# Pacing the first forty loads of an attention and feed-forward kernel: eight in flight or three

## The chip, the cores and the metric

The kernel runs on one core of a Trainium2 chip. The metric is the device time of one execution in microseconds, lower is better. A core has TensorE (matrix products), VectorE, ScalarE, GpSimd, and SyncE, which here only issues DMA transfers; sixteen DMA engines move the data. Each engine works through its own instructions in order, and engines wait for each other, and for transfers, by semaphores.

## The reference

Attention in two forms on 8 batches of 8 heads (576 positions, head size 64), their sum taken as 4608 tokens of 512 numbers, and a feed-forward block with `h * cos(h)` in the middle. Cut to what matters:

```python
q_d, k_d, v_d = (a.reshape(B, H, S // 4, 4, D).mean(axis=3) for a in (q, k, v))
out_up = np.repeat(sm_attn(q_d, k_d, v_d), 4, axis=2)          # attention on 144 positions
mask = np.abs(pos[:, None] - pos[None, :]) < 4                 # and within three positions
scores = np.where(mask, scale * q @ k.T, -1e9)
out_local = softmax(scores) @ v
x = (out_up + out_local).transpose(0, 2, 1, 3).reshape(4608, 512)
h = x @ w_in                                                   # 512 -> 2048
return (h * np.cos(h)) @ w_out                                 # 2048 -> 512
```

The weights come in float64.

## The kernel before

**Work and stages.** The attention is cut into 32 units, one for each of the 8 batches and 4 pairs of heads. A unit loads q and k (128 x 584 numbers, 292 KB each), v for the averaged form (`vdn`, 288 KB on 72 partitions) and v for the local form (`vl`, 384 KB); then come scores, softmax, transposes and the product with v. The five steps are `u_qk`, `u_v`, `u_s`, `u_t` and `u_pv`. The feed-forward part takes tokens in 12 tiles of 384 and the 2048 inner columns in 16 chunks of 128. Each chunk has one load of `w_in` (`wdi`, 512 KB) and one of `w_out` (`wdo`, 512 KB) in `w_load`, and `w_split` turns the float64 bits into two float32 parts, on ScalarE first (L412) and then on VectorE and GpSimd. `gemm1` (L731) and `gemm2` (L767) are the two products. The first three token tiles go through the chunks in four groups of four, so that the products can begin before all weights are there; the other nine take all chunks at a time.

**What sets the order.** A planner (`Plan`) records every step with an estimate of its length, schedules all steps by list over the engines, and then emits the instructions in that order. The loads have an order by hand: q and k of batch 0 (loads 1 to 8), v of its first two head pairs (9 to 12), weight chunk 0 (13, 14), v of the other pairs (15 to 18), chunk 1 (19, 20), q and k of batch 1 (21 to 28), chunk 2 (29, 30), v of batch 1 (31 to 38), and so on; load 40 is the first q of batch 2. Batches 0 and 1 use memory that later holds weights, so their tiles appear as wxi, wxo and xxl in the rows.

**What the change and the rows touch.** All transfers that SyncE issues pass the helper `dma` (L382 to L385): weights at L402, q and k at L468, vdn at L489, vl at L490, and also moves of `ptb` (L631) and stores of results (L789), which come after the first forty. Of the readers, L482 (VectorE) and L475 and L477 (GpSimd) sum q or k over four positions, L496 and L497 do so for v, and L538 and L547 are the score products. L884 are dummy products that keep TensorE busy in the early part.

**Semaphores.** The framework below the planner puts the waits in. A SyncE transfer signals one of eight semaphores in turn, DMAHW0 to DMAHW7, and before one is taken again SyncE waits for the transfer that had it: at most eight are in flight.

Of the kernel before, what the change touches and what calls it, by code (L numbers as in the profile page):

```python
# [49 lines left out]
ON_PE = ()  # L50
BOOST = {0: 100.0}
LAG = 2
PI = math.pi


# [22 lines left out]
class Plan:  # L78
# [47 lines left out]
    def part(self, parent, off, n, make):  # L126

        b = self.buf(make)
        b.parent, b.prev = parent, []
        for lo, hi, p in parent.parts:  # L130
            if lo < off + n and off < hi:
                b.prev.append(p)
        parent.parts = [x for x in parent.parts if not (off <= x[0] and x[1] <= off + n)] + [(off, off + n, b)]
        return b
# [152 lines left out]
def _act(n, psum=True, extra=0):  # L287
    return n * 0.000833 + (0.051 if psum else 0.093) + 0.093 * extra


def _dve(n):
    return n * 0.001042 + 0.065
# [7 lines left out]
def attn_ffn_kernel(ctx: ExitStack, tc: tile.TileContext, qT, kT, vdn, vl, w_in, w_out, out):  # L300
# [8 lines left out]
    pl = Plan()  # L309

    def sb(tag, n, shape, dtype=F32, name=None, pool=None):
        t = pl.turn(tag, n)
        return pl.buf(lambda: (pool or ap).tile(shape, dtype, name=name or tag, tag=t, bufs=1), t)
# [63 lines left out]
    w_dram = {"i": w_in.bitcast(I32).rearrange("(a p) (f t) -> p a f t", p=P, t=2),  # L377
              "o": w_out.bitcast(I32).rearrange("f (n t) -> f n t", t=2)}

    loads = {}  # L380

    def dma(nbytes, fn, r=(), w=(), pw=()):  # L382
        o = pl.op("SP", max(0.45, nbytes / 262e3), fn, r=r, w=w, pw=pw, lat=1.8)
        loads.setdefault((pl.name,) + pl.arg, []).append(o)
        return o  # L385

# [7 lines left out]
    def w_load(k, c):  # L394
        pl.name = "w_load"
        wd = words[(k, c)]
        if k == "i":
            src = lambda: w_dram["i"][:, :, c * P:(c + 1) * P, :]
            dst = lambda: wd.get().rearrange("p (a f) t -> p a f t", a=KC)
        else:  # L400
            src, dst = (lambda: w_dram["o"][c * P:(c + 1) * P]), wd.get
        dma(4096 * P, lambda: sp.dma_start(dst(), src()), w=[wd])  # L402
# [58 lines left out]
    def u_qk(b, pr):  # L461
        pl.name = "u_qk"
        q, k, qkd = (ub(b, pr, n) for n in ("q", "k", "qkd"))
        s4 = [lambda: q.get()[:, 0:S].rearrange("p (a r) -> p a r", r=4), lambda: k.get()[:, PAD:PAD + S].rearrange("p (a r) -> p a r", r=4)]
        early = b < NEARLY
        bk = bank(b, "t") if early and ON_PE else None
        for i, (src, ram) in enumerate(((q, qT), (k, kT))):
            dma(4 * P * SP_, lambda src=src, ram=ram: sp.dma_start(src.get(), ram[b, pr]), w=[src])  # L468

            def on_pe(i=i):  # L470
                for r in range(4):
                    pe.matmul(bk.get()[:, i * SD:(i + 1) * SD], ident, s4[i]()[:, :, r], start=(r == 0), stop=(r == 3))

            def on_pool(i=i):
                pool.tensor_tensor(out=qkd.get()[:, i], in0=s4[i]()[:, :, 0], in1=s4[i]()[:, :, 1], op=ALU.add)  # L475
                for r in (2, 3):
                    pool.tensor_tensor(out=qkd.get()[:, i], in0=qkd.get()[:, i], in1=s4[i]()[:, :, r], op=ALU.add)  # L477
            if early and i in ON_PE:
                pl.op("PE", 4 * _mm4(SD), on_pe, r=[src], pw=[bk])
                evac(SD, lambda i=i: qkd.get()[:, i], lambda i=i: bk.get()[:, i * SD:(i + 1) * SD], bk, qkd)  # L480
            else:
                pl.op("DVE", _dve(S), lambda i=i: dve.tensor_reduce(out=qkd.get()[:, i], in_=s4[i](), axis=AX.X, op=ALU.add),  # L482
                      r=[src], pw=[qkd], alts=[("POOL", 3 * _pool(2 * SD), on_pool)])
        st[(b, pr)] = dict(q=q, k=k, qkd=qkd)

    def u_v(b, pr):
        pl.name = "u_v"
        vd4, vt = ub(b, pr, "vd4"), ub(b, pr, "vl")
        dma(16 * P * HD * 2, lambda: sp.dma_start(vd4.get(), vdn[b, pr].rearrange("p a r n -> p (a r) n")), w=[vd4])  # L489
        dma(4 * P * 12 * D, lambda: sp.dma_start(vt.get(), vl[b, pr]), w=[vt])  # L490
        vd = ub(b, pr, "vd")
        v4 = lambda: vd4.get().rearrange("p (a r) n -> p a r n", a=2)

        def v_add(e):
            def f():
                e.tensor_tensor(out=v4()[:, :, 0:2, :], in0=v4()[:, :, 0:2, :], in1=v4()[:, :, 2:4, :], op=ALU.add)  # L496
                e.tensor_tensor(out=vd.get(), in0=v4()[:, :, 0, :], in1=v4()[:, :, 1, :], op=ALU.add)  # L497
            return f
        pl.op("POOL", 2.2, v_add(pool), w=[vd, vd4], alts=[("DVE", 1.1, v_add(dve))], shares=True)
        st[(b, pr)].update(vd=vd, vl=vt)  # L500

    def u_s(b, pr):
# [96 lines left out]
        for sm, part, size in ((sml, sul, n), (smd, sud, m)):  # L599
            if not (early and sm is smd):  # L600
                pl.op("DVE", _dve(size), lambda sm=sm, part=part: dve.tensor_reduce(  # L601
                    out=part(), in_=sm.get(), axis=AX.X, op=ALU.add), r=[sm, su], pw=[su2])
        pl.op("DVE", 0.1, lambda: dve.tensor_scalar(out=su.get(), in0=su.get(), scalar1=1e-9, scalar2=2.0 * PI,
                                                    op0=ALU.add, op1=ALU.mult), r=[su2], w=[su])
# [114 lines left out]
    def gemm1(t, c):  # L719
# [15 lines left out]
        tr = sb("tr", 4, [P, m], pool=fp)  # L735
        gh, gl = sb("gh", LAG + 1, [P, m], F32R, pool=fp), sb("gl", LAG + 1, [P, m], F32R, pool=fp)
        h = lambda: ph.get()[:, :m]

        def sin2():
            act.activation(tr.get(), tr.get(), AF.Sin, scale=PI)  # L740
            act.activation(tr.get(), tr.get(), AF.Square)  # L741
# [13 lines left out]
    def gemm2(t, c, c0, c1):  # L755
# [19 lines left out]
        for i in range(SIZE[t] // P):  # L775
# [4 lines left out]
            if c == c1 - 1:  # L780
                bk, ob = accs[i], sb("tr", 4, [P, DM], name="ob", pool=fp)

                pl.op("ACT", _act(DM), lambda bk=bk, ob=ob: act.activation(ob.get(), bk.get(), AF.Copy, scale=-4.0 * PI),
                      r=[bk], w=[ob], alts=[("DVE", _dve(DM), lambda bk=bk, ob=ob: dve.tensor_scalar(
                          out=ob.get(), in0=bk.get(), scalar1=-4.0 * PI, scalar2=None, op0=ALU.mult))])
                dst = out[FROM[t] + i * P:FROM[t] + (i + 1) * P, :]
# [11 lines left out]
    def at(t, f, *a):  # L798
        ev.append((t, len(ev), f, a))

    def unit(t, step, ahead, *a):
        for d, f in ((-ahead, u_qk), (0.01 - ahead, u_v), (0.0, u_s), (step, u_t), (2 * step, u_pv)):
            at(t + d, f, *a)
# [23 lines left out]
    for b in range(2, B):  # L827
        t0, t1 = tile_of(b * S), tile_of(b * S + S - 1)
        lo, hi = (done[t1 - NX] if t1 >= NX else 0), first[t0]
        for i in range(NPAIR):  # L830

            last = max(lo - 2.5 + (hi - lo - 1.0) * i / (NPAIR - 1), last + 1.5)
            unit(last, 1.4, 2.5, b, i)
    for i in range(len(steps) + LAG):
        if i < len(steps):
            at(i, gemm1, *steps[i][:2])
        if i >= LAG:
            at(i + 0.5, gemm2, *steps[i - LAG])
    for t, i, f, a in sorted(ev, key=lambda e: e[:2]):
# [85 lines left out]
```

## Time and profile before

| what | value |
|---|---|
| median of 3 runs | 1016.51 us (1007.5 to 1016.57) |
| profiled execution, its own time | 1012.63 us |
| span of the profiled execution | 1010.8 us |
| TensorE busy | 984.4 us (97%) |
| VectorE, ScalarE, GpSimd busy | 679.4, 610.4, 220.2 us |
| DMA | 80.70 MB, mean 80 GB/s |
| mean granted TensorE clock | 0.986 |

The span runs from the first to the last instruction of one profiled execution. A row of the timeline gives start and length in microseconds, engine, line, operation and tiles; a bracket behind it gives the idle time of that engine just before and what ended it. SPq is SyncE's queue, where the length is that of the issue and not of the transfer; PE is TensorE, DVE is VectorE, ACT is ScalarE, POOL is GpSimd. A row by stretches gives, for each engine, busy microseconds and instructions, then the granted share of TensorE's clock, the mean busy share of the DMA engines, and what they moved.

### The profile page before, as it was taken

How to read it: one execution, taken by the hardware profiler on the slowest of the kernel's cores; microseconds unless marked ns; L12 is line 12 of the kernel's file. 1: busy time of each engine (PE TensorE's matmuls, PEld its weight loads, DVE VectorE, ACT ScalarE, POOL GpSimd, SP SyncE). 2: the span in 40 equal slices, each digit the busy share in tenths (PEclk: the TensorE clock that was granted, in tenths of full speed). 3: DMA queues.
4: the chain of work that ended last, by engine and by line, in shares of the span. 5: the costliest groups of instructions: out<-in, count | busy, mean ns of one | idle time of the engine just before them, and what ended most of it. 6: DMA issues, size and time to landing. Idle time of an engine off the chain costs nothing.

```text
span 1010.8 us, 23855 instructions
## 1 busy us (share of the span) xinstructions
PE 984.4 (97%) x9917; PEld 849.5 (84%) x9917; DVE 679.4 (67%) x1362; ACT 610.4 (60%) x1174; POOL 220.2 (22%) x280
## 2 busy tenths in 40 slices
PE   7888999999999999999999999999999999999998
PEld 4556799899887888888888888888898888899997
DVE  6599899996487678564748866655657875433433
ACT  2457688876576656555647655655646755655554
POOL 5676324623144202100003211200001300000000
PEclk9998799999999999999999999999999999999999
DMA  9753651524255422211212321201112320100000
GB/s 279 232 198 96 231 208 41 86 48 70 52 124 123 83 61 83 67 29 32 67 49 75 121 64 52 88 26 36 58 57 64 112 73 1 40 1 1 32 1 32
DMA packets 41051, 80.70 MB, mean 80 GB/s; under 512 B 4976, under 2 KB 16240, under 8 KB 40944
## 3 DMA queue, kind: packets, MB, share of 16 engines
q1 hardware_dynamic: 37056, 72.11, 22.8%
q0 software_dynamic: 3888, 7.08, 4.9%
q8 instruction: 78, 1.28, 0.5%
q14 instruction: 29, 0.24, 0.1%
HBM read 57.93 MB, written 16.52 MB: 74 GB/s over the span
## 4 chain that ended last, share of the span: by engine, by line
PE 88%; DVE 5%; DMA 3%; POOL 1%; issue 1%; SPq 1%; ACT 1%; ACTq 0%; DVEq 0%; POOLq 0%
PE bank L767 38%; PE bank L731 38%; PE bank L531 2%; PE bank L547 2%; PE bank L676 2%; PE bank L657 2%; PE bank L884 2%; PE bank L640 1%; DMA q<-qT 1%; DMA wdi<-w_in 1%; PE bank L669 1%; PE bank L538 1%; SPq L631 1%; DVE su L601 0%; DMA ptb<-sml 0%
## 5 line engine op out<-in xcount | busy, mean ns | idle before, releaser
L767 PE MATMUL bank<-wo,gh 128*128 128x512 f32 x1152 | 363.6, 396 | 0.0
L767 PEld LDWEIGHTS bank<-wo,gh 128*128 128x128 f32 x1152 | 210.0, 188 | 38.0 <-issue 3.3
L767 PE MATMUL bank<-wo,gl 128*128 128x512 f32 x576 | 227.6, 395 | 0.0
L742 ACT ACTIVATE tr<-bank,bmagic 128x384 f32<-128x384 f32 x192 | 110.9, 577 | 114.7 <-PE bank L731 110.8
L746 DVE SCALAR_TENSOR_TENSOR tr<-tr,bank 128x384 f32<-128x384 f32 x192 | 104.9, 546 | 107.9 <-ACT tr L741 107.1
L743 DVE SCALAR_TENSOR_TENSOR tr<-tr,bank 128x384 f32<-128x384 f32 x192 | 105.7, 550 | 85.2 <-ACT tr L742 84.3
L740 ACT ACTIVATE tr<-tr 128x384 f32<-128x384 f32 x192 | 100.7, 524 | 76.3 <-DVE tr L743 75.7
L748 ACT ACTIVATE gh<-tr 128x384 fp32r<-128x384 f32 x163 | 85.3, 523 | 87.1 <-DVE tr L746 85.5
L391 DVE TENSOR_TENSOR gl<-tr,gh 128x384 fp32r<-128x384 f32 x154 | 92.4, 600 | 63.5 <-ACT gh L748 60.5
L767 PEld LDWEIGHTS bank<-wo,gl 128*128 128x128 f32 x576 | 108.0, 188 | 23.5
L731 PE MATMUL bank<-x0h,wi 128*128 128x384 f32 x384 | 108.0, 342 | 0.0
L731 PE MATMUL bank<-x1h,wi 128*128 128x384 f32 x384 | 107.3, 340 | 0.0
L731 PE MATMUL bank<-x2h,wi 128*128 128x384 f32 x384 | 106.8, 339 | 0.0
L731 PE MATMUL bank<-x3h,wi 128*128 128x384 f32 x384 | 106.5, 338 | 0.0
L741 ACT ACTIVATE tr<-tr 128x384 f32<-128x384 f32 x192 | 100.8, 525 | 6.1
L391 POOL TENSOR_TENSOR gl<-tr,gh 128x384 fp32r<-128x384 f32 x38 | 43.2, 1137 | 268.7 <-DVE gh L749 175.1
L731 PEld LDWEIGHTS bank<-x0h,wi 128*128 128x128 f32 x384 | 70.9, 190 | 2.7 <-DVE mxd L574 0.4
L731 PEld LDWEIGHTS bank<-x1h,wi 128*128 128x128 f32 x384 | 70.6, 189 | 2.6 <-issue 0.6
L731 PEld LDWEIGHTS bank<-x2h,wi 128*128 128x128 f32 x384 | 70.2, 188 | 2.3 <-issue 0.4
L731 PEld LDWEIGHTS bank<-x3h,wi 128*128 128x128 f32 x384 | 70.2, 188 | 2.0
L731 PE MATMUL bank<-x0l,wi 128*128 128x384 f32 x192 | 65.0, 339 | 1.0 <-DVE x0l L391 1.0
L731 PE MATMUL bank<-x1l,wi 128*128 128x384 f32 x192 | 64.7, 337 | 0.0
(199 smaller groups left out, 1452.9 us busy)
## 6 DMA issues: line engine op xcount, KB each, us to landing
vl<-vl SPq DMA_DIRECT2D x26, 384.0 KB
out<-ob SPq DMA_DIRECT2D x36, 256.0 KB
wdi<-w_in SPq DMA_DIRECT2D x16, 512.0 KB
wdo<-w_out SPq DMA_DIRECT2D x16, 512.0 KB
q<-qT SPq DMA_DIRECT2D x26, 292.0 KB
k<-kT SPq DMA_DIRECT2D x26, 292.0 KB
vd<-vdn SPq DMA_DIRECT2D x26, 288.0 KB
out<-ob POOLq DMA_DIRECT2D x27, 256.0 KB, 5.2
```

Of the source, the lines that this page charges most:

```text
L391: f = lambda e: lambda: e.tensor_tensor(out=out(), in0=in0(), in1=in1(), op=ALU.subtract)
L531: pe.matmul(banks[h].get()[BS * g:BS * (g + 1), c:c + BS], q.get()[hs, o:o + BS], k.get()[hs, o:o + BS], start=True, stop=True)
L547: pe.matmul(banks[h].get()[:HD, i * SD:(i + 1) * SD], qkd.get()[hs, 0, i * HD:(i + 1) * HD], qkd.get()[hs, 1, :], start=True, stop=True)
L657: pe.matmul(banks[0].get()[64 * h:64 * h + 64, 2 * SD:3 * SD], vd.get()[:, kh, 64 * h:64 * h + 64], ptd.get()[:, h, kh, :], start=(kh == 0 ...
L731: pe.matmul(ph.get()[:, :m], w[:, i, kc, :], x[:, kc, :], start=(n == 0), stop=(n == 3 * KC - 1))
L740: act.activation(tr.get(), tr.get(), AF.Sin, scale=PI)
L741: act.activation(tr.get(), tr.get(), AF.Square)
L742: pl.op("ACT", _act(m, True, 1), lambda: act.activation(tr.get(), h(), AF.Identity, bias=bmagic), r=[ph], w=[tr])
L743: pl.op("DVE", _dve(m), lambda: dve.scalar_tensor_tensor(out=tr.get(), in0=tr.get(), scalar=MAGIC, in1=h(), op0=ALU.subtract, op1=ALU.subt ...
L746: pl.op("DVE", _dve(m), lambda: dve.scalar_tensor_tensor(out=tr.get(), in0=tr.get(), scalar=0.5, in1=h(), op0=ALU.subtract, op1=ALU.mult), ...
L748: pl.op("ACT", _act(m, False), lambda: act.activation(gh.get(), tr.get(), AF.Copy), r=[tr], w=[gh], alts=[("DVE", _dve(m / 2), lambda: dve ...
L767: pe.matmul(o, (gh, gh, gl)[k].get()[:, sl], wo.get()[:, (0, 1, 0)[k]], start=(c == c0 and k == 0), stop=(c == c1 - 1 and k == 2))
```

## The change

Each of the first forty loads, from the fourth on, gets a dependence on the load three places ahead of it in the order of issue. SyncE waits for that load's semaphore and then issues. From load 41 on the framework's own waits are all there is. The order of instructions on each engine stays as it was.

```diff
+AHEAD, FIRST = 3, 40
...
-    loads = {}
+    loads, begun = {}, []
 
     def dma(nbytes, fn, r=(), w=(), pw=()):
-        o = pl.op("SP", max(0.45, nbytes / 262e3), fn, r=r, w=w, pw=pw, lat=1.8)
+        def begin():
+            ins = fn()
+            if ins is not None and len(begun) < FIRST:
+                if len(begun) >= AHEAD:
+                    tc.add_manual_dep(ins.ins, begun[-AHEAD].name, mybir.DependencyInfo(
+                        mybir.DependencyClass.Sync, mybir.DependencyReason.DATA), reason="loads in flight")
+                begun.append(ins.ins)
+        o = pl.op("SP", max(0.45, nbytes / 262e3), begin, r=r, w=w, pw=pw, lat=1.8)
         loads.setdefault((pl.name,) + pl.arg, []).append(o)
         return o
```

SyncE's queue at the start of the program, before the change, is as follows. The number behind a tile's name tells buffers apart, and the bracket names the semaphores that the issue waits for.

```order
L468 DMA q<-qT 128x584
L468 DMA k<-kT 128x584
L468 DMA wxi_132<-qT 128x584
L468 DMA wxo_136<-kT 128x584
L468 DMA wxo_197<-qT 128x584
L468 DMA wxi_200<-kT 128x584
L468 DMA wxi_214<-qT 128x584
L468 DMA wxo_273<-kT 128x584
L489 DMA vd_281<-vdn 72x1024 [waits DMAHW0_49]
L490 DMA vl<-vl 128x768 [waits DMAHW1_49]
L489 DMA wxi_308<-vdn 72x1024 [waits DMAHW2_49]
```

The same place on SyncE after the change (lines stand eight further down in the changed file):

```order
L476 DMA q<-qT 128x584
L476 DMA k<-kT 128x584
L476 DMA wxi_132<-qT 128x584
L476 DMA wxo_136<-kT 128x584 [waits DMAHW0_49]
L476 DMA wxo_197<-qT 128x584 [waits DMAHW1_49]
L476 DMA wxi_200<-kT 128x584 [waits DMAHW2_49]
L476 DMA wxi_214<-qT 128x584 [waits DMAHW3_49]
L476 DMA wxo_273<-kT 128x584 [waits DMAHW4_49]
L497 DMA vd_281<-vdn 72x1024 [waits DMAHW5_49]
L498 DMA vl<-vl 128x768 [waits DMAHW6_49]
L497 DMA wxi_308<-vdn 72x1024 [waits DMAHW7_49]
```

No row moved. The wait of load 9 was on load 1 and is on load 6, and loads 4 to 8 have a wait where they had none.

SyncE's queue around load 40 before the change, with buffers to be free (PE_49, Pool_49) among the waits:

```order
L490 DMA wxo_585<-vl 128x768 [waits DMAHW5_49,PE_49]
L402 DMA wdi_1049<-w_in 128x4x256 [waits DMAHW6_49]
L468 DMA q<-qT 128x584 [waits DMAHW7_49,Pool_49]
L468 DMA k<-kT 128x584 [waits DMAHW0_49]
L402 DMA wdo_1163<-w_out 128x1024 [waits DMAHW1_49]
L402 DMA wdi_1175<-w_in 128x4x256 [waits DMAHW2_49]
L402 DMA wdo_1202<-w_out 128x1024 [waits DMAHW3_49]
```

And the same place after the change:

```order
L498 DMA wxo_585<-vl 128x768 [waits DMAHW2_49,PE_49]
L410 DMA wdi_1049<-w_in 128x4x256 [waits DMAHW3_49]
L476 DMA q<-qT 128x584 [waits DMAHW4_49,Pool_49]
L476 DMA k<-kT 128x584
L410 DMA wdo_1163<-w_out 128x1024
L410 DMA wdi_1175<-w_in 128x4x256
L410 DMA wdo_1202<-w_out 128x1024
```

Load 40 (q) waits for load 37 in place of load 32, and loads 41 to 45 need no wait of their own any more, since the loads eight ahead of them are known to have landed.

## The prediction

> **What bounds the kernel now.** I read the page's shares first, then the work by stretches of time, then SyncE's queue (where the change is made), and last the instructions that use the loads. The page, engines and chain:
>
> ```profile
> span 1010.8 us, 23855 instructions
> PE 984.4 (97%) x9917; PEld 849.5 (84%) x9917; DVE 679.4 (67%) x1362; ACT 610.4 (60%) x1174; POOL 220.2 (22%) x280
> PE 88%; DVE 5%; DMA 3%; POOL 1%; issue 1%; SPq 1%; ACT 1%; ACTq 0%; DVEq 0%; POOLq 0%
> ```
>
> TensorE is busy 97% of the span, so a change can reach at most 1010.8 - 984.4 = 26.4 us of idle time there, and that busy time includes dummy matmuls early on. The view by stretches (per engine busy us and count, then granted clock, DMA share, GB/s) shows where the idle lies:
>
> ```profile
> 0.00:5.00 5.00, 3.63 (x16) 1.15 (x20) 1.38 (x3) 1.28 (x1) 3.90 (x16) 1.00 0.63 196
> 5.00:10.00 5.00, 5.00 (x206) 3.04 (x206) 2.74 (x8) 0.02 (x1) 4.32 (x16) 1.00 1.03 350
> 20.00:25.00 5.00, 5.00 (x73) 2.81 (x67) 2.35 (x7) 0.61 (x2) 0.39 (x1) 0.66 1.03 250
> 30.00:35.00 5.00, 4.38 (x118) 2.74 (x117) 4.96 (x13) 3.31 (x14) 1.72 (x2) 1.00 1.01 360
> 35.00:40.00 5.00, 4.13 (x51) 2.16 (x49) 5.00 (x12) 1.85 (x5) 2.53 (x4) 1.00 0.68 197
> 40.00:60.00 20.00, 16.44 (x346) 10.21 (x339) 13.63 (x23) 6.42 (x15) 18.25 (x27) 0.91 0.30 87
> 120.00:1011.00 891.00, 884.14 (x7876) 783.19 (x7874) 585.84 (x1175) 550.84 (x1008) 151.65 (x173) 1.00 0.23 63
> ```
>
> From 120 us on TensorE idles only 6.9 us in 891; the first sixty microseconds hold the forty loads, and the DMA engines are full (share 1.0) from 5 to 35 us. So the change acts where the transfers are saturated, and reaches the end only through what waits for a load there.
>
> SyncE's queue before, as the timeline has it (start, length, instruction):
>
> ```profile
> 0.74 0.39 SPq L468 DMA_DIRECT2D q<-qT  x1
> 1.65 0.43 SPq L468 DMA_DIRECT2D wxi<-qT  x1
> 2.12 0.43 SPq L468 DMA_DIRECT2D wxo<-kT  x1
> 4.02 0.54 SPq L468 DMA_DIRECT2D wxo<-kT  x1
> 5.76 0.32 SPq L489 DMA_DIRECT2D wxi<-vdn  x1
> 7.20 0.33 SPq L490 DMA_DIRECT2D wxo<-vl  x1
> 7.92 0.38 SPq L402 DMA_DIRECT2D wdi<-w_in  x1
> 8.66 0.34 SPq L402 DMA_DIRECT2D wdo<-w_out  x1
> 9.57 0.32 SPq L489 DMA_DIRECT2D wxo<-vdn  x1
> 10.86 0.33 SPq L490 DMA_DIRECT2D wxi<-vl  x1
> 22.14 0.33 SPq L468 DMA_DIRECT2D xxl<-qT  x1
> 57.54 0.32 SPq L489 DMA_DIRECT2D wxi<-vdn  x1
> 58.85 0.46 SPq L468 DMA_DIRECT2D q<-qT  x1
> ```
>
> The kernel is already paced, at eight: load n+8 waits for the semaphore of load n, so where nothing else holds it, the issue of load n+8 tells when load n landed. Load 11 went out at 5.76, so load 3 landed then; loads 4 to 8 landed at 7.20, 7.92, 8.66, 9.57 and 10.86. That is (10.86 - 5.76) / 5 = 1.02 us for each load of 292 KB, with eight in flight. Loads land in the order of their issue: what stands behind a load in the queue seems to cost it little.
>
> **What pacing at three does to each load.** No instruction is added on any compute engine and none moves; SyncE's forty issues each wait for a nearer load. The consumers, as the timeline has them, with the idle time and its releaser in brackets:
>
> ```profile
> 3.68 0.75 DVE L482 TENSOR_REDUCE qkd<-q 128x144 f32<-128x576 f32 x1 [2.81 <-DMA q<-qT]
> 4.37 0.76 DVE L482 TENSOR_REDUCE qkd<-k 128x144 f32<-128x576 f32 x1
> 5.76 0.75 DVE L482 TENSOR_REDUCE wxi<-wxi 128x144 f32<-128x576 f32 x1 [0.64 <-DMA wxi<-qT]
> 7.30 0.74 POOL L515 MEMSET ptb<- 128x768 f32 x1
> 9.81 1.03 POOL L475 TENSOR_TENSOR wxo<-wxi 128x144 f32<-128x144 f32 x1
> 12.08 0.56 POOL L475 TENSOR_TENSOR wxi<-wxo 128x144 f32<-128x144 f32 x1
> 15.69 1.26 POOL L496 TENSOR_TENSOR wxi<-wxi 72x512 f32<-72x512 f32 x1 [1.56 <-DMA wxi<-vdn]
> 19.06 0.12 POOL L559 MEMSET su<- 128x16 f32 x1 [1.32 <-DVE su L603]
> 27.09 1.27 POOL L496 TENSOR_TENSOR wxo<-wxo 72x512 f32<-72x512 f32 x1
> 55.99 0.66 ACT L412 ACTIVATE xxh<-wdi 128x512 f32<-128x512 f32 x1 [0.81 <-DVE wo L391]
> 71.61 0.62 POOL L475 TENSOR_TENSOR qkd<-q 128x144 f32<-128x144 f32 x1
> ```
>
> Round trip: load 1 was issued at 0.74 and used at 3.68, 2.94 us with an empty queue. Load 3, with two in front, took 5.76 - 1.65 = 4.11 us. These bound a load that starts with two ahead of it: three loads per 2.94 us (0.98 each) to three per 4.11 us (1.37 each), against 1.02 with eight in flight. I take 1.1, nearer to the lower end, because of load 3's 4.11 us some part was spent behind loads 1 and 2 at the very start of the stream.
>
> Step by step:
> - **Loads 1 to 3** go out as before: 0.
> - **Loads 4 to 8.** Load 4 is issued at 3.7 in place of 2.12 and lands at 3.7 + 2.94 to 4.11 = 6.6 to 7.8 (before 7.20). GpSimd, which needs it, is clearing ptb until 7.30 + 0.74 = 8.04, so 0. Load 6 goes out when load 3 has landed, 5.8, and lands at 8.7 to 9.9 (8.66); GpSimd uses it at 9.81: 0 to +0.1. Load 8 follows load 5, which lands at 7.3 to 8.5, so 10.3 to 12.6 (10.86), used at 12.08: 0 to +0.5.
> - **Load 11** is the one load after the third that an engine waited for: it landed by 15.69 and GpSimd had idled 1.56 us. By trips from load 8 it lands between 10.3 + 2.94 = 13.2 and 12.6 + 4.11 = 16.7: 1.6 us earlier is no use, since GpSimd idles again before 19.06 (1.32 us); up to +1.0 late is covered by that same 1.32 us. If that cover were gone it would cost +1.0.
> - **Loads 12 to 36.** Load 15 landed at 22.14 (when load 23 went out) and is used at 27.09, 5.0 us of slack. From load 3 it is four trips of three loads: 5.76 + 4 x 4.11 = 22.2 even at the long trip, so 0. Load 29, the third w_in chunk, stands nine trips after load 2 (used 4.37): at most 4.4 + 9 x 4.11 = 41.4, or with two longer trips for its 512 KB loads some 44, and is used at 55.99: 0. Loads 31 to 38 also wait for buffers, and DMA share in 40 to 60 us is 0.30; pacing costs nothing in an idle queue.
> - **Load 40** (q of batch 2) waits for load 37, issued at 57.54: 60.5 to 61.7 in place of 58.85. Behind it on SyncE stand loads 41 to 47, six weight loads and k, which slip by 1.6 to 2.8 us at issue. Loads 38 and 39, 384 and 512 KB, still move then, so the engines have work. The first user is GpSimd at 71.61, 10 us on: 0.
> - **A gain** can come from load 3's 0.64 us on VectorE, if nothing behind it competes any more: -0.6 to 0.
>
> The Trainium skill, "DMA: Bandwidth & Descriptors", section "Anatomy of one DMA", fits one transfer as about 2.0 us plus its bytes at 436 GB/s. By it a 292 KB load would take an estimated 2.7 us, and three in flight 0.9 us each: the trace's 2.94 for the lone load nearly agrees, and the sum stays at zero. The same page's "Rules for kernel authors" advises issuing early and waiting late, so that the fixed part overlaps; it speaks against this change, and it is the second rival's mechanism.
>
> Sum: -0.6 to +1.6 (0.1 + 0.5 + 1.0), of which I take +0.3 us, since the covers named above are all seen in the trace. The profiled execution took 1012.63 us (span 1010.8 and 1.8 around it); so 1012.9. That stands 3.9 below the median 1016.51 of three runs that lie at 1007.50, 1016.51 and 1016.57, so between the two levels of the kernel. I predict **1014 us**, between that sum and the median.
>
> **What else a lighter queue could touch.** TensorE stalls that nothing in the profile ended ("issue") might be instruction fetch behind the loads:
>
> ```profile
> 19.49 0.99 PE L538 MATMUL bank<-wxo,wxi 64*32 64x32 f32 x85 [2.65 <-issue]
> 47.81 0.67 PE L669 MATMUL bank<-wxi,wxo 32*64 32x24 f32 x32 [2.54 <-issue]
> ```
>
> One falls in the full stretch, the other in the stretch with share 0.30, and they differ by 0.1 us: they don't depend on the queue, and I book nothing.
>
> **Rivals.** *Faster by clock windows.* After idle gaps TensorE is granted half its clock for some microseconds:
>
> ```profile
> 77.52 0.41 PE L640 MATMUL bank<-ident,wxi 72*72 72x72 f32 x4 [1.90 <-DVE wxi L607]
> 79.00:86.00 7.00, 6.93 (x102) 5.51 (x91) 7.00 (x14) 5.46 (x15) 4.54 (x7) 0.51 0.14 43
> 105.77 0.84 PE L640 MATMUL bank<-ident,wxi 72*72 72x72 f32 x8 [1.68 <-DVE wxi L607]
> 106.40:116.60 10.20, 10.20 (x220) 7.10 (x218) 8.46 (x18) 3.62 (x10) 1.66 (x3) 0.50 0.49 161
> ```
>
> 10.2 us at half clock with TensorE busy throughout cost up to 5.1 us, the 7 us before them 3.4. If shifted loads moved the gaps, both could go: 1012.6 - 8.5 = 1004; the later one alone, 1007.5. For it: the sizes resemble the 9 us between the runs. Against: both gaps end on VectorE, 15 us and more behind the last paced load. The Trainium skill, "TensorE: Matmul & The Clock Gate", Part 1, says that the half rate follows an idle window of about 3.4 us of a free-running counter; here gaps of 1.7 to 1.9 us precede it, so the trace does not bear out the length. A free-running window would make this chance, alike for both kernels. Chance 10% for a move of 4 us or more down by it, 7% for the same up (1017 to 1021).
>
> *Slower: three in flight don't cover the round trip.* Place: the stream of loads 4 to 36. If a trip costs 6.5 us per three loads in place of at most 4.11 (long landing confirmations under load), load 29 lands at 4.4 + 9 x 6.5 = 62.9 and ScalarE's split at 55.99 waits 6.9 us, with the first products behind it: 1019.5. It decides from (55.99 - 4.4) / 9 = 5.7 us per trip, and costs over 1% from 6.9. For it: the DMA engines run at only 250 GB/s in 20 to 25 us with eight in flight. Against: load 3's 4.11 us with two others in flight. Chance 6%.
>
> *Faster because early loads no longer share.* If a load alone at the head lands sooner, load 3's 0.64 and load 11's 1.56 us vanish: 1012.6 - 2.2 = 1010.4 if all of it reached the end, though the cover at 19.06 takes the second. 7%. *The pacing doesn't act*: SyncE's rows show the waits at three back, so 1%.
>
> **Numbers.** No change beyond noise 69%, the rivals as given. A per cent is 10 us, about what the runs of this kernel differ by without any change, and nearly all cases lie within it: faster by over 1%: 0.03 (both clock windows gone and the sum below zero), within 0.92, slower 0.05 (most of the second rival's upper part, and an added clock window from the upper level). The range takes the lower level 1007.5 with the gain and a part of a clock window, 1005.5, to the upper level 1016.6 with the sum's upper end and a clock window of 3.4 us at half, 1020.
>
> **What would show it.** In the profile after: at most three loads in flight, load 4 issued near 3.7 us; GpSimd at its load 6 and 8 rows within 0.5 us of 9.81 and 12.08; load 29's split near 56 with no DMA as releaser; and stretches after 120 us unchanged. Wrong if ScalarE or GpSimd idle on a DMA for over 2 us before 60 us, if DMA throughput in 5 to 35 us falls by a third, or if the half-clock stretches after 79 us come or go.

## The result, and the profile after

The changed kernel takes 1006.62 us (median of 20 runs), the kernel before 1014.7 us in runs beside it: a ratio of 0.9931, 95% interval 0.9914 to 0.9947. One of its 20 runs, at 1888.57 us, fell in a slow state and is left out of the ratio. That is 7 us less, within the predicted range and within one per cent, but a clear gain where the sum had none. Page of the changed kernel (shares, engines, chain):

```profile
span 1005.6 us, 23855 instructions
PE 981.2 (98%) x9917; PEld 847.3 (84%) x9917; DVE 681.7 (68%) x1362; ACT 610.2 (61%) x1174; POOL 221.3 (22%) x280
...
PE 87%; DVE 6%; DMA 4%; issue 1%; ACT 1%; SPq 0%; ACTq 0%; DVEq 0%
```

The view of the changed kernel by stretches, with the columns explained earlier:

```profile
5.00:10.00 5.00, 4.22 (x206) 2.60 (x206) 3.66 (x10) 0.55 (x2) 4.32 (x15) 1.00 0.88 255
20.00:25.00 5.00, 4.33 (x118) 2.75 (x117) 4.13 (x12) 2.97 (x9) 1.27 (x5) 1.00 0.75 245
30.00:35.00 5.00, 3.29 (x54) 2.06 (x58) 5.00 (x11) 1.94 (x5) 2.71 (x4) 1.00 0.71 205
40.00:60.00 20.00, 15.10 (x216) 9.04 (x214) 15.73 (x30) 8.35 (x25) 14.68 (x21) 0.82 0.79 225
120.00:1011.00 891.00, 878.64 (x7848) 778.11 (x7847) 580.39 (x1168) 545.88 (x999) 146.33 (x167) 1.00 0.23 62
```

The DMA engines moved less from 5 to 10 and from 30 to 35 us (255 and 205 GB/s where it was 350 and 360), hardly less from 20 to 25 us (245 and 250), and more between 40 and 60 us (225 and 87). Over the whole stretch from 5 to 35 us they moved 235 GB/s where it was 318, which is 26% less. SyncE's queue in the changed kernel, where the issue of load n+3 tells the landing of load n unless a buffer holds it longer:

```profile
3.56 0.33 SPq L476 DMA_DIRECT2D wxo<-kT  x1
10.23 0.38 SPq L497 DMA_DIRECT2D vd<-vdn  x1
11.76 0.32 SPq L497 DMA_DIRECT2D wxi<-vdn  x1
17.65 0.34 SPq L410 DMA_DIRECT2D wdo<-w_out  x1
24.67 0.34 SPq L498 DMA_DIRECT2D wxo<-vl  x1
47.42 0.34 SPq L498 DMA_DIRECT2D vl<-vl  x1
59.87 0.33 SPq L476 DMA_DIRECT2D q<-qT  x1
```

The rows are the issues of loads 4, 9, 11, 14, 18, 32 and 40. So load 8 landed at 11.8 (10.86 before), load 11 at 17.7 (by 15.69), load 15 at 24.7 (22.14) and load 29 at 47.4. The loads came later, and the kernel got faster all the same.

Most of where the time came from is in TensorE's rows, and one row of VectorE. The first kernel's two stalls on nothing visible were shown; these are the two others that it has before 55 us:

```profile
12.39 1.47 PE L884 MATMUL bank<-ident_b 128*128 128x512 bf16 x6 [0.68 <-issue]
27.53 1.48 PE L669 MATMUL bank<-sml,vl 32*64 32x24 f32 x89 [0.80 <-issue]
29.04 0.31 DVE L458 TENSOR_SCALAR xd<-bank 128x144 f32<-128x144 f32 x1 [6.25 <-PE bank L669]
```

All such stalls of the changed kernel in that stretch, and the same VectorE instruction:

```profile
15.79 0.99 PE L546 MATMUL bank<-wxo,wxi 64*32 64x32 f32 x85 [0.50 <-issue]
37.68 0.68 PE L546 MATMUL bank<-k,q 64*32 64x32 f32 x56 [0.29 <-issue]
41.52 0.66 PE L677 MATMUL bank<-wxi,wxo 32*64 32x24 f32 x32 [0.88 <-issue]
22.74 0.31 DVE L466 TENSOR_SCALAR xd<-bank 128x144 f32<-128x144 f32 x1
```

Before, 0.68 + 2.65 + 0.80 + 2.54 = 6.67 us; after, 0.50 + 0.29 + 0.88 = 1.67. VectorE no longer waits 6.25 us for TensorE, and its first instruction behind that wait starts 6.3 us earlier. By then the stalls account for 4.13 - 0.50 = 3.63 us of this lead. Another 1.6 us lies between two rows where TensorE was granted half its clock before the change (0.66 on the mean of 20 to 25 us) and all of it after. Before the change:

```profile
20.95 1.20 PE L547 MATMUL bank<-wxi 64*72 64x144 f32 x8
25.12 0.84 PE L657 MATMUL bank<-ptd,vd 72*64 72x144 f32 x8
```

The same two in the changed kernel, 2.56 us apart in place of 4.17:

```profile
17.25 0.71 PE L555 MATMUL bank<-wxi 64*72 64x144 f32 x8
19.81 0.84 PE L665 MATMUL bank<-ptd,vd 72*64 72x144 f32 x8
```

The difference of the stalls, 5.0 us, is close to the difference of the spans, 5.2, but that is in part a coincidence: over the whole span TensorE's busy time fell by 3.2 us (984.4 to 981.2) and its idle time by only 2.0 (26.4 to 24.4), so other waits grew.

Not all of the lead is kept. In the changed kernel GpSimd waits for a v load (load 33), and some ten microseconds later instructions of VectorE take longer than before:

```profile
53.99 1.61 POOL L504 TENSOR_TENSOR wxi<-wxi 72x512 f32<-72x512 f32 x1 [4.30 <-DMA wxi<-vdn]
63.41 1.64 DVE L399 TENSOR_TENSOR wxi<-wxi,mxl 128x384 f32<-128x384 f32 x1
64.97 1.49 DVE L423 TENSOR_SCALAR xxh<-xxh 128x512 int32<-128x512 int32 x1
68.38 0.54 DVE L609 TENSOR_REDUCE su<-wxi 128x12 f32<-128x384 f32 x1
```

The same three instructions of VectorE before the change:

```profile
70.45 0.60 DVE L391 TENSOR_TENSOR wxi<-wxi,mxl 128x384 f32<-128x384 f32 x1
70.97 0.96 DVE L415 TENSOR_SCALAR xxh<-xxh 128x512 int32<-128x512 int32 x1
73.69 0.54 DVE L601 TENSOR_REDUCE su<-wxi 128x12 f32<-128x384 f32 x1
```

VectorE leads by 70.45 - 63.41 = 7.0 us here, and by 5.3 three microseconds on; the spans differ by 5.2. That GpSimd's late work is what stretches these instructions was not tested: GpSimd was at work beside VectorE here in both kernels.

The waits for loads that the changed kernel has on ScalarE and GpSimd are these (in us: in total, number, longest); before, GpSimd had one of 1.56 us and ScalarE none:

```profile
ACT xxh L420 <- DMA wdi<-w_in: 4.8, 2, 2.7
POOL wxi L504 <- DMA wxi<-vdn: 7.7, 2, 4.3
```

### The profile page after: what moved, and what is told of

It is laid out like the page before. It is cut to its first block, busy times and chain, and to the rows that moved or that the text cites. A ratio compares the mean times of both kernels' runs of the same rounds, so it can differ in the third digit from the quotient of the medians.

```text
span 1005.6 us, 23855 instructions
## 1 busy us (share of the span) xinstructions
PE 981.2 (98%) x9917; PEld 847.3 (84%) x9917; DVE 681.7 (68%) x1362; ACT 610.2 (61%) x1174; POOL 221.3 (22%) x280
## 3 DMA queue, kind: packets, MB, share of 16 engines
q8 instruction: 78, 1.28, 0.5%
## 4 chain that ended last, share of the span: by engine, by line
PE 87%; DVE 6%; DMA 4%; issue 1%; ACT 1%; SPq 0%; ACTq 0%; DVEq 0%
PE bank L775 38%; PE bank L739 38%; PE bank L539 2%; PE bank L684 2%; PE bank L555 2%; PE bank L665 2%; PE bank L648 1%; DMA q<-qT 1%; DMA wdi<-w_in 1%; PE bank L892 1%; PE bank L677 1%; DMA vl<-vl 1%; DVE su L609 1%; DMA wxi<-qT 0%; DVE wxo L615 0%
## 5 line engine op out<-in xcount | busy, mean ns | idle before, releaser
L399 DVE TENSOR_TENSOR gl<-tr,gh 128x384 fp32r<-128x384 f32 x154 | 92.4, 600 | 63.5 <-ACT gh L756 60.5
L739 PE MATMUL bank<-x3l,wi 128*128 128x384 f32 x192 | 64.6, 336 | 0.0
```

Source lines behind the costliest of these rows:

```text
L399: f = lambda e: lambda: e.tensor_tensor(out=out(), in0=in0(), in1=in1(), op=ALU.subtract)
L739: pe.matmul(ph.get()[:, :m], w[:, i, kc, :], x[:, kc, :], start=(n == 0), stop=(n == 3 * KC - 1))
```

## What the stalls are

In both traces TensorE's weight loads and products were counted in the order of their start. In the kernel before it stalls ahead of its instructions 449, 705, 961 and 1985, and in the changed one ahead of 705, 1729 and 1985: all stand a multiple of 256 apart. The DMA records have a queue of its own for instructions; of both kernels the page has this row:

```profile
q8 instruction: 78, 1.28, 0.5%
```

78 packets of 1.28 / 78 MB = 16.4 KB would be 64 bytes for each of 256 instructions, and TensorE's 19,981 instructions make 78 such pages. Each stall ends 1.3 to 1.6 us after a packet of this queue does:

| kernel | page begins at instruction | TensorE entered the page before | packet starts, ends | TensorE goes on | from entering to packet start |
|---|---|---|---|---|---|
| before | 449 | 6.04 | 9.44, 10.83 | 12.39 | 3.4 us |
| before | 705 | 12.39 | 16.87, 17.95 | 19.49 | 4.5 |
| before | 961 | 19.49 | 25.05, 26.16 | 27.53 | 5.6 |
| before | 1985 | 42.32 | 45.40, 46.42 | 47.81 | 3.1 |
| after | 705 | 10.52 | 12.99, 14.22 | 15.79 | 2.5 |
| after | 1729 | 34.73 | 35.36, 36.38 | 37.68 | 0.6 |
| after | 1985 | 37.68 | 38.83, 40.05 | 41.52 | 1.2 |

The table has only the pages that TensorE had to wait for. Over all eight pages whose predecessor was entered between 5 and 50 us, the time from entering to packet start was 2.9 us on the mean before the change (from -0.1 to 5.6) and 1.5 after (0.6 to 2.5).

So theory A: TensorE's next page is asked for when it enters the one before, and the request stands behind the packets of loads that are already queued on the DMA engines. The trace shows the time and not the queue, so the second half is inferred, from how the time falls with the depth. Where TensorE runs through 256 short instructions in less than that, it stands still. The rivals: **B**, the first loads land sooner or are served more evenly, which the landings above already speak against; **C**, the clock windows fell better.

## The experiments

All are edits of one of the two kernels; unless a diff says otherwise it is of the changed one. The stall column adds up TensorE's waits on nothing visible between 5 and 55 us of the profiled execution. Runs went to different chips, and each ratio is to the kernel before on the same chip: median 1012.88 us beside the first four experiments, 1014.69 beside the next four, 1013.51 beside the last two.

Each run has its mean granted TensorE clock on record, and runs of one kernel differ by it. Of 73 runs of the kernel before beside the experiments, the 20 with a clock of 0.974 to 0.980 have a median of 1015.4 us and the 12 with 0.987 to 0.991 one of 1009.5. So the last column is an estimate, fitted to the lists of runs, of the difference to the kernel before at the same granted clock (with two standard errors); a run took 0.5 to 0.7 us less for each thousandth of clock. What a change does to the clock itself is in the ratio and not in this column.

| run | stalls, us | median, us | ratio to the kernel before, 95% interval | us at equal clock, estimate |
|---|---|---|---|---|
| kernel before | 6.67 | 1014.7 | 1 | 0 |
| changed kernel | 1.67 | 1006.62 | 0.9931 (0.9914 to 0.9947) | no clock on record beside it |
| only loads 4 to 20 paced | 6.01 | 1010.06 | 0.998 (0.9964 to 0.9996) | -2.5 ± 0.7 |
| only loads 21 to 40 paced | 5.92 | 1012.18 | 0.999 (0.9967 to 1.0014) | -0.9 ± 0.8 |
| five in flight | 5.52 | 1011.33 | 0.9987 (0.9966 to 1.0008) | -1.4 ± 0.7 |
| two in flight | 1.76 | 1016.71 | 1.004 (1.0023 to 1.0057) | +2.8 ± 0.8 |
| before, few small products | 0 | 1001.52 | 0.9879 (0.9858 to 0.99) | -10.8 ± 1.4 |
| changed, few small products | 0 | 1001.12 | 0.9878 (0.9857 to 0.9899) | -10.7 ± 1.4 |
| changed kernel again | 1.45 | 1006.27 | 0.9931 (0.9907 to 0.9955) | -4.5 ± 1.8 |
| three in flight, to load 30 | 1.32 | 1004.34 | 0.9908 (0.989 to 0.9925) | -5.3 ± 2.0 |
| before, pages shifted | 10.32 | 1014.47 | 1.0011 (0.9987 to 1.0035) | +3.1 ± 1.1 |
| four in flight, to load 30 | 4.07 | 1009.87 | 0.9962 (0.9936 to 0.9988) | -2.0 ± 1.1 |

At equal clock the whole kernels follow the stall column, which is of one execution each. Against the 6.67 us of the kernel before, the changed kernel again has 5.2 us of stalls less and is 4.5 us faster, three in flight to load 30 has 5.4 less and is 5.3 faster, four has 2.6 less and is 2.0 faster, five has 1.2 less and is 1.4 faster, the late half has 0.8 less and is 0.9 faster, and with the pages shifted it has 3.7 more and is 3.1 slower. Two runs do not follow: the early half alone gains more than its stalls, and two in flight is slower with fewer stalls, for the reason given there.

**One half of the loads at a time.**

```diff
-AHEAD, FIRST = 3, 40
+AHEAD, FIRST = 3, 20
```

> Only loads 4 to 20 are paced at three; from load 21 on eight may be in flight again. Theory A (TensorE's instruction pages come by the same DMA engines as the loads, and a shorter queue lets them through sooner): the stalls of TensorE before 30 us stay short (0.5 us in all after the change, 4.1 before), the one at 45 us may come back (2.5 us before, 0.9 after), and the late v loads no longer hold GpSimd for 4.3 us near 50 us, so 4 to 8 us under the kernel before. Theory B (the first loads land sooner, or the engines serve them more evenly): all of the gain, 7 us, and loads 4 to 20 land no later than before. Theory C (the clock windows fell better): the time follows the sum of half-clock time after 70 us, and the stalls don't matter.

Measured: 0.998, some 2 us. The stalls before 25 us are gone, as A has it, but three longer ones came behind, where the queue fills again:

```profile
26.96 1.24 PE L677 MATMUL bank<-wxi,wxo 32*64 32x24 f32 x72 [1.60 <-issue]
40.24 0.97 PE L546 MATMUL bank<-k,q 64*32 64x32 f32 x56 [2.12 <-issue]
47.66 1.06 PE L677 MATMUL bank<-wxi,wxo 32*64 32x24 f32 x32 [2.29 <-issue]
```

A's size was too large, since it looked for one stall to return and three did. B, which expected all of the gain here, is refuted: the first twenty loads are paced exactly as in the changed kernel, and most of the gain is missing.

```diff
-                if len(begun) >= AHEAD:
+                if len(begun) >= 20:
```

> Only loads 21 to 40 are paced at three. Theory A: the stalls before 30 us are back (4.1 us, and the 6 us idle of VectorE near 29 us with them), the one near 45 us falls from 2.5 to about 1, the late v loads hold GpSimd; so within 2 us of the kernel before. Theory B: no gain, since the first loads go out as before. Theory C: no prediction but that half-clock time and total go together.

Measured: no difference that can be told (0.999). The early stalls are back (0.67 and 2.92 us), as A says. Its late ones add up to 2.33 us, hardly less than the 2.54 before. Neither half alone has the gain: in the run with the early half paced, what is saved early is paid at later pages, where eight may be in flight again.

**Other depths.**

```diff
-AHEAD, FIRST = 3, 40
+AHEAD, FIRST = 5, 40
```

> All forty paced at five in flight. Theory A: the page that TensorE waits for spends between 2 us (three in flight) and 4.5 us (eight) in the queue, so the stalls before 50 us add up to 2 to 4 us in place of 6.7 or 1.7; the v loads land earlier than at three, and GpSimd waits less than 4.3 us for load 33: 3 to 8 us under the kernel before. Theory B: about half of the gain, 3 to 4 us.

Measured: 0.9987, nothing that can be told, where A expected 3 to 8 us and stalls of 2 to 4 us (5.52 measured). The stall ahead of instruction 705, 3.20 us, is no shorter than with eight in flight. Over the pages entered before 50 us a packet starts 2.7 us on the mean after the page before is entered, where it was 2.9 with eight: five loads of 288 to 512 KB still hold it up.

```diff
-AHEAD, FIRST = 3, 40
+AHEAD, FIRST = 2, 40
```

> All forty paced at two in flight. Theory A: TensorE's stalls fall to under 1.7 us in all, but loads take two per 3.5 to 4.5 us, so load 29 lands near 60 us where it was needed at 48 to 56: 0 to 8 us slower than the kernel before. Theory B (sooner first loads): if fewer in flight make the first loads land sooner, at least the gain of three, 7 us.

Measured: 4 us slower (1.004), as A has it. Stalls are short, 1.76 us, of which 0.75 does not stand at a page; a packet starts 1.5 us on the mean after the page before is entered, no sooner than with three. But now the engines wait for the loads themselves:

```profile
39.34 0.68 ACT L420 ACTIVATE xxh<-wdi 128x512 f32<-128x512 f32 x1 [4.75 <-DMA wdi<-w_in]
57.96 0.67 ACT L420 ACTIVATE xxh<-wdi 128x512 f32<-128x512 f32 x1 [1.92 <-DMA wdi<-w_in]
65.16 2.33 POOL L504 TENSOR_TENSOR wxi<-wxi 72x512 f32<-72x512 f32 x1 [7.16 <-DMA wxi<-vdn]
```

**Hardly a page to wait for.** In each of the two kernels the small products of batches 0 and 1 are replaced by a few wide ones; the attention of these two batches is therefore not the reference's, and TensorE has some 2800 instructions less. The score products (the value products likewise):

```diff
-            for n in range(2 * NSEG):
+            for g in range(2):
                 for h in range(2):
-                    for e in range(2):
-                        ...
-                        pe.matmul(banks[n // NSEG].get()[64 * h + BS * e:64 * h + BS * (e + 1), c:c + BS],
-                                  q.get()[hs, o:o + BS], k.get()[hs, o:o + BS], start=True, stop=True)
+                    hs = slice(64 * h, 64 * h + 64)
+                    pe.matmul(banks[g].get()[hs, LQ:LQ + NSEG * BS], q.get()[hs, 0:64], k.get()[hs, 0:NSEG * BS],
+                              start=True, stop=True)
```

> The kernel before, with eight loads in flight, but the small products of batches 0 and 1 are left out: 48 score products of 32x32 and 48 value products of 64x24 for each unit are replaced by 4 wide ones each, so the attention of these two batches is not what the reference asks. That takes some 350 TensorE instructions out of each of 8 units, so that in the first 50 us TensorE crosses two or three pages of 256 instructions and not eight. Theory A (waits for instruction pages): stalls in the first 50 us under 1.5 us although eight loads are in flight. Theory C or any that does not rest on pages: nothing special.

> The changed kernel (forty loads at three in flight) with the same small products left out. Theory A: with hardly a page to wait for, pacing has nothing to win, and the later loads remain, so this is equal to the thinned kernel with eight in flight or up to 5 us slower. Theory B (loads land better) and theory C (clock windows): about 7 us faster than it, as with the whole kernels.

Measured: 1001.52 us with eight in flight and 1001.12 with three, ratios 0.9879 and 0.9878 on the same chip. The gain of pacing is gone when there are few pages to fetch, at equal clock too (-10.8 and -10.7 us), which B and C do not explain. With eight in flight the whole list of TensorE's waits before 55 us has no stall of the kind left (longest first: us in total, times, longest):

```profile
PE bank L639 <- ACT smd L612: 4.9, 1, 4.9
PE bank L639 <- DVE wxo L606: 1.7, 1, 1.7
PE bank L880 <- POOL ident_b masks.py:199: 1.4, 1, 1.4
PE bank L546 <- POOL wxi L477: 1.0, 1, 1.0
PE bank L639 <- DVE vd L684: 0.6, 1, 0.6
PE bank L727 <- DVE x0l L391: 0.2, 1, 0.2
```

The requests were not quicker: two of them stood 2.5 and 2.7 us before their packets began. TensorE just did not need the page for 17 us and more.

**The pages moved.** The kernel before, with 64 tiny products at the start:

```diff
         constants()
+        for _ in range(64):
+            pe.matmul(first[:32, :32], ident_b[:32, :32], ident_b[:32, :32], start=True, stop=True)
+        fewer = 3
 ...
-                for _ in range(max(n, CFG["warm"] if ahead else 0)):
+                for _ in range(max(n, CFG["warm"] if ahead else 0) - fewer):
                     pe.matmul(s[2].get(), ident_b, ident_b.unsqueeze(1).broadcast_to([P, 4, P]), start=True, stop=True)
                 last = o.start + o.dur
+                fewer = 0
```

> The kernel before, eight in flight, with 64 tiny dummy products at the start of TensorE's program (and three of the wide dummies fewer), so that every later instruction stands 122 places further on and the page boundaries, every 256 instructions, fall 122 instructions earlier in the work. Theory A: the stalls are still 256 instructions apart counted from the start, and so at other products: not after the first 11 of the fourth unit's score products and not after 7 of the first value products, as before, but between the score products of the second to fourth unit, and inside other value products; their length stays 0.7 to 3 us. Any theory that ties the stalls to the data of these products: they stay where they were. The time may go either way by some us.

Measured: the stalls stand ahead of instructions 449, 705 and 961 again, which are now other products:

```profile
13.14 0.96 PE L538 MATMUL bank<-wxo,wxi 64*32 64x32 f32 x51 [4.21 <-issue]
19.73 0.53 PE L538 MATMUL bank<-wxi,wxo 64*32 64x32 f32 x37 [1.37 <-issue]
27.56 0.53 PE L538 MATMUL bank<-wxo,wxi 64*32 64x32 f32 x19 [4.74 <-issue]
```

They fall into the score products of the second, third and fourth unit. Before, only the fourth was cut, after 11 of 96. Two are longer than A expected, and TensorE now reaches the first page sooner (at 8.9 us in place of 11.7). The stalls add up to 3.7 us more, and yet the median is the same within the interval. The clock on record tells why: these ten runs were granted more of it (median 0.9855) than the 23 of the kernel before beside them (0.983), and at equal clock the shifted kernel is 3.1 us slower.

**The changed kernel again, and a better one.**

> The changed kernel itself, on the chip of this call. All theories: 0.993 of the kernel before, within 0.002.

Measured: 0.9931, as expected. The medians differ by 8.4 us here, and the granted clock by 0.986 to 0.981; at equal clock 4.5 us are left. So an estimated 3 to 4 us of this difference came with a higher granted clock.

```diff
-AHEAD, FIRST = 3, 40
+AHEAD, FIRST = 3, 30
```

> Pacing at three ends with load 30, when the last page wait of the early stretch is over (near 41 us). Theory A: stalls as after the change (1.7 us in all), and loads 31 to 38 move in a fuller queue, so GpSimd's wait of 4.3 us near 50 us shrinks to about 2: 1 to 3 us under the changed kernel. Theory B: as the changed kernel, since the first thirty loads are the same.

Measured: 1004.34 us, ratio 0.9908; stalls 1.32 us, and GpSimd's wait for load 33 near 50 us is 1.33 us in place of 4.30. It is the fastest whole kernel here and clearly faster than the kernel before; against the changed kernel (1006.27 on the same chip) the intervals overlap, and at equal clock the two are 0.8 us apart (-5.3 and -4.5).

```diff
-AHEAD, FIRST = 3, 40
+AHEAD, FIRST = 4, 30
```

> Four in flight, up to load 30. Theory A: page waits between those of three (0.5 us before 30 us) and five (3.5 us), while the loads land earlier; 0.992 to 0.998 of the kernel before, so not better than three in flight up to load 30 (0.991). Were the best depth set by the landing of loads alone, it would be faster than that.

Measured: 0.9962, within A's range: 4.07 us of stalls, 1.66 of them at 23.78.

## Why the prediction was right or wrong, point by point

- **"Only through what waits for a load there."** The prediction let the change reach the end only that way, and this is the root of its error. It left out that another kind of transfer uses the DMA engines: TensorE's own instructions. Its bound by TensorE's idle time did not hold either, since busy time fell too, by 3.2 us.
- **The stalls named "issue".** The step that failed. It set a stall of 2.65 us in the full stretch beside one of 2.54 us in a stretch with a mean DMA share of 0.30, found them alike, and booked nothing. The mean over 20 us hid that two loads (33 and 34, issued at 41.47 and 41.89) were moving when the second page was asked for, at 42.3: the DMA share was 0.40 from 40 to 45 us and 0.53 from 45 to 50. The step should have had about -5 us, which is what the profile shows (6.67 to 1.67).
- **The trip of three loads.** Mis-sized: bounded by 4.11 us, it came to (47.42 - 4.42) / 9 = 4.8 us from load 2 to load 29. So load 11 (17.7, bound 16.7), load 15 (24.7, bound 22.2) and load 29 (47.4, bound 41 to 44) were all later than the working allowed. The fit that the prediction quotes from the Trainium skill, "DMA: Bandwidth & Descriptors", section "Anatomy of one DMA", is given there for transfers issued by GpSimd, and these are issued by SyncE; its estimate of 0.9 us a load of 292 KB compares with 1.6 measured over loads of 288 to 512 KB.
- **The covers** held for loads 6 and 8 (used at 10.28 and 12.49, predicted to within 0.5 us of 9.81 and 12.08) and for load 29 (used at 48.44). They did not hold elsewhere. GpSimd waited 3.38 us for load 11, 0.63 for load 15 and 4.30 for load 33, and ScalarE 2.14 and 2.71 us for loads 13 and 19. The early ones took nothing from the lead: behind them TensorE's first product of `gemm1` starts at 47.61 in place of 53.85, 6.2 us earlier. For load 33 the text had said that pacing cost nothing in an idle queue; the queue was not idle any more, since earlier loads had moved into it. The lead falls from 7.0 to 5.3 us between 63 and 68 us, behind this wait; how much of that is its doing no run shows.
- **Load 3's gain** of up to 0.6 us came: VectorE's wait of 0.64 us for it is gone.
- **Load 40** went out at 59.87 (predicted 60.5 to 61.7) and held nobody, as predicted.
- **Rivals.** *Three in flight too slow*: not at three, where 4.8 us a trip is below the 5.7 that decide; the run with two shows the mechanism, at 4 us slower. *Earlier landing of the first loads*: refuted, they land later. *Clock windows*: in part. The 3.4 us at half clock near 21 us, behind the stall of 2.65 us, are gone and gave 1.6 us; the 7 us at 79, one of the two stretches that this rival named, are gone as well, and a new 10.2 us stand at 56.2. The 10.2 us near 106 are there in both (now at 100.6). Before 120 us the half-clock time is 27.3 us before and 23.9 after. More on this rival stands below the list.
- **The predicted time**, 1014, was the kernel without the 5 to 8 us. That the result lies in the range is luck: the range was made wide for the spread between runs, its lower end of 1005.5 is only 1.1 us below the result, and the cause that it had in mind there was the clock and not the pages. (In its sum, 1012.9 stands 3.6 and not 3.9 us below the median; nothing hangs on it.)
- **The signs named in advance**: two of the three for "wrong" came. GpSimd and ScalarE idled on a load for over 2 us, and the half-clock stretch at 79 us went. Throughput from 5 to 35 us fell by 26%, less than the third that was named.

The rows of 75 to 95 us, before and then after, show the half clock that went (the clock is the third number from the end):

```profile
75.00:95.00 20.00, 16.78 (x358) 12.39 (x358) 19.19 (x35) 15.16 (x35) 13.21 (x16) 0.83 0.17 51
75.00:95.00 20.00, 16.95 (x311) 13.21 (x299) 19.12 (x38) 14.11 (x33) 13.20 (x15) 1.00 0.29 83
```

Over many runs an estimated 3 to 4 of the 8.4 us between the changed kernel again and the kernel before go with the clock. The other 4.5 remain at equal clock, and the thinned pair shows no gain that is independent of the pages. A part of the clock's share may come from the stalls themselves. In the four profiled executions with a stall of 2.65 us or more before 20 us (the kernel before, the late half, five in flight, pages shifted) half clock begins between 12.9 and 21.0 us, during that stall or up to 1.6 us behind it; in the other eight it begins at 24.4 us or later. Against it stands the run with the pages shifted, which has the longest stalls and yet a higher clock over its ten runs than the kernel before.

## What to carry to other kernels

A queue of loads kept deep is not free: here TensorE's instructions came as DMA packets too, and its stretches of many short products needed a page every 2 to 9 us. TensorE stalls named "issue" that stand a multiple of 256 instructions apart were pages on their way; look at what was queued when the page before was entered, not at the mean DMA share of the stretch. Depth is then a trade: three loads in flight here saved 5 us of stalls, five saved nothing that the ratio shows, and two starved the engines of data. Ending the pacing at load 30 gave the lowest median, but not clearly. And before two medians are compared, set their granted clocks side by side: here five thousandths of clock were worth an estimated 3 to 4 us.

## What was not expected of the hardware

With eight loads in flight a packet of instructions started 2.9 us on the mean, and up to 5.6, after TensorE entered the page ahead of it; with three it was 1.5 us, and up to 2.5. From the packet's end to TensorE's next instruction it took another 1.2 to 1.7 us at the page stalls of all runs. The Trainium skill, "Runtime: NRT & Kernel Launch", section "Instruction fetch mechanics", has the 16 KiB blocks of 256 instructions, which these traces bear out, and calls the cost of crossing one mostly hidden; here single crossings cost up to 4.74 us.

Left open: whether the depth counts by loads or by bytes, and what else holds a packet up (the page asked for at 42.3 us before the change took 3.1 us with two loads on their way); how much of the higher granted clock is an effect of the shorter stalls; and what sets the clock of a single run. No run was made on these.
